# Folding each batch's memory values into the first mixture's weights, with attention weights as its input

## The chip, the cores and the metric

One Trainium2 chip, one of its cores. The metric is the device time of one execution in microseconds. An execution of this kernel has five engines at work: TensorE (PE, with its weight loads shown as PEld), VectorE (DVE), ScalarE (ACT), GpSimd (POOL), and SyncE (SP), which here only issues transfers.

## The reference, cut to what matters

Three parts follow each other: a memory attention of 4 batches of 576 tokens (8 heads of 64), a gated mixture layer of 1536 columns over all 2304 tokens, and a second layer that sends every token to two of eight experts.

```python
a = softmax(phi)                                   # 32 memories per head
k_m = einsum('bhsm,bhsd->bhmd', a, k)
v_m = einsum('bhsm,bhsd->bhmd', a, v)
attn = softmax(q @ k_m.T / 8)                      # tokens x 32 memories, per head
x = (attn @ v_m).transpose(0, 2, 1, 3).reshape(2304, 512)
x = (sigmoid(x @ w_gate) * (x @ w_val)) @ w_out    # first mixture
x = top2_experts(x)                                # second mixture
```

With 8 heads of 32 memories, the attention weights of a token are 256 numbers; the values that they are multiplied with differ from batch to batch only. Nothing non-linear stands between `attn @ v_m` and the two products with `w_gate` and `w_val`.

## The kernel before, in words

Numbers that stand for fp32 are kept as two f16 parts, hi and lo, and a product is three f16 matmuls (hi hi, hi lo, lo hi). The parts come from `split` (line 391): a ScalarE copy with a scale (392) and a VectorE subtraction (393).

*Attention* (lines 166 to 315) works batch by batch in fp32: `memory` builds the keys and values of the memories, four heads beside each other on the array (187), `scores` and `turned` the attention weights with their tokens on the columns (244, 265), `result` the product with the values (278, 285), whose hi and lo are `xT[b]` (288, 289), 512 rows by 576 tokens. Attention is a generator, `atts`; the main loops take a step of it after each piece of their own work.

*Weights* (343 to 389) arrive as 64-bit words, 36 halves of 512 KB through four buffers, and are put together by ScalarE, VectorE and GpSimd (337 to 341). Gate and value weights are split into hi and lo, 12 blocks of 128 x 1024 (`finish`, 350 to 358). Those of w_out are split last (385 to 389), after all have been summed.

*First product*, `stage1` (426 to 453): for a chunk c of 256 tokens and a tile f of 128 columns, 2 x 12 matmuls of up to 256 columns (442) into one PSUM buffer of four (`pg`), where chunks that straddle a batch are cut in two. Then Tanh on ScalarE (448), a VectorE step (449), a ScalarE copy (451) and a VectorE subtraction (452) give gT in hi and lo. There are 9 x 12 calls.

*Second product*, `stage2` (455 to 464): for each tile T of 128 tokens 36 matmuls of 512 columns into `px`. `tokens` (466) then scales and stores the row, transposes it by a transfer (482, 485), multiplies it with the router (492) and, for every second tile, `route` (546) computes the choice and scatters it to the table `meta` (608).

*Order in `build`* (989 to 1079): the first three chunks of the first product are computed beside the weights, 36 calls; then come the second product of chunk 0 and, in turn, a call of the first product and a third of a tile of the second (1057 to 1068). Presplits of the first experts' weights (632 to 677) run beside it once attention is done, and are drained before the last chunk. After chunk 6 the routing is frozen for the first three tiles of expert 0 (615 to 623), which are fetched, gathered and transposed (755 to 777, 814) under the last chunk's first product. The end of the first mixture is two second products (1072), the early rows' matmuls (1074), and the fetch of the late rows (1079, 1080). A scheduler orders the instructions of each engine at build time by priority and dependence.

*Second mixture*, `moe2`, lines 786 and 800, isn't touched.

Of the kernel before, what the change touches and what calls it, by code (L numbers as in the profile page):

```python
# [26 lines left out]
P = 128  # L27
# [5 lines left out]
NCH = N // CH  # L33
NT = N // P
# [12 lines left out]
FB = 8  # L47
SG = 3

STEPS = 3  # L50

GT = 36
WAIT_W, WAIT_SPLIT, WAIT_TURN, WAIT_ROUTE = 2, 4, 5, 4
WAIT_TURN_LAST, WAIT_ROUTE_LAST = 4, 2
# [7 lines left out]
class Kern:  # L62
# [12 lines left out]
    def norm2(self, pool, m, tag, before=1, n=1):  # L75
# [11 lines left out]
        nc.vector.tensor_scalar(h, pt.bitcast(I32), 24, 23, op0=ALU.logical_shift_right, op1=ALU.logical_shift_left)  # L87
        nc.vector.tensor_scalar(s, h, -1, 204 << 23, op0=ALU.mult, op1=ALU.add)
# [3 lines left out]
    def consts(self):  # L92
# [10 lines left out]
        self.idle = cp.tile([P, 256], F16, name="idle")  # L103
        nc.vector.memset(self.idle, 0.0)
        self.ones = cp.tile([P, P], F16, name="ones")
        nc.vector.memset(self.ones, 1.0)

    def warm(self, n):

        nc = self.nc  # L110
        pt = self.pg.tile([P, 512], F32, tag="pg", name="pw")
        for i in range(n):
            d = nc.tensor.matmul(pt[:, :256], self.ones, self.idle, start=True, stop=True)
            self.tc.add_manual_dep(d.ins, self.mark.ins.name, mybir.DependencyInfo(mybir.DependencyClass.NoSync, mybir.DependencyReason.DATA), reason="order")
            self.mark = d


    def att_open(self):
        tc, nc = self.tc, self.nc
        self.att_ctx = ExitStack()  # L120
        pool = lambda name, bufs: self.att_ctx.enter_context(tc.tile_pool(name=name, bufs=bufs, side="left"))
        self.stage = pool("stage", 4)
        self.a1 = pool("a1", 1)
        self.a2 = pool("a2", 2)
        self.kbds = [self.a1.tile([P, 4, 64], F32, name=f"kbd{i}") for i in range(1)]
        self.vbds = [self.a1.tile([P, 4, P], F32, name=f"vbd{i}") for i in range(1)]
        for t in self.kbds + self.vbds:
            nc.gpsimd.memset(t, 0.0)
        self.al, self.ag = {}, {}

    def att_load(self, b, what, g):
# [5 lines left out]
        else:  # L137
            if what == "q" and b == 0:
                t = self.flat(self.xp.tile([P, KT, S], F16, tag=f"x{g}", name=f"x{g}")).bitcast(F32)
            else:  # L140
                t = self.stage.tile([P, (SC + 1) * 256], F32, tag="st", name="st")
            if what == "q":
                t = t[:, : 2 * S].rearrange("p (t s) -> p t s", t=2)
                src = a["q"][b * DM : (b + 1) * DM, :].rearrange("(g t p) s -> g p t s", p=P, g=2)[g]
# [21 lines left out]
    def memory(self, b, g):  # L166

        nc, a2, al = self.nc, self.a2, self.al
        kbd, vbd = self.kbds[0], self.vbds[0]
# [18 lines left out]
        km = a2.tile([P, 2, D], F32, tag="km", name="km")  # L188
        nc.scalar.copy(km, pm[:, :D].unsqueeze(1).to_broadcast([P, 2, D]))
        for j in range(4):  # L190
            rows = slice(32 * j, 32 * j + 32)
            nc.scalar.copy(vbd[rows, 2 * g + j // 2, (j % 2) * 64 : (j % 2) * 64 + 64], pm[rows, D:])
# [3 lines left out]
        pk = self.pg.tile([P, 512], F32, tag="pg", name="pa")[:, :P]  # L196
        nc.tensor.transpose(pk, km.rearrange("p a d -> p (a d)"), self.idf)
        pk = pk.rearrange("p (a b) -> p a b", a=2)
        for j in range(2):
            rows, cols = slice(64 * j, 64 * j + 64), slice(32 * j, 32 * j + 32)  # L200
            nc.scalar.copy(kbd[rows, 2 * g : 2 * g + 2, cols], pk[rows, :, cols])
# [18 lines left out]
    def values_scale(self, b):  # L220
        m = self.a2.tile([P, 1], F32, tag="vm", name="vm")
        self.xT[b] = [self.xp.tile([P, KT, S], F16, tag=f"x{i}", name=f"x{i}") for i in range(2)]
        junk = self.xT[b][0][:, 0, :512].bitcast(BF16)
        self.nc.scalar.activation(junk, self.flat(self.vbds[0]), AF.Square, accum_out=m)
        self.sv[b], iv = yield from self.norm2(self.cp, m, f"sv{b}")
        self.invx.append(iv)

    def attention(self, b):

        nc, a2, al, sv = self.nc, self.a2, self.al, self.sv[b]  # L230
        kbd, vbd = self.kbds[0], self.vbds[0]
        qt = [al[(b, "q", g)] for g in range(2)]
        def scores(u):
# [3 lines left out]
            for pr in range(2):  # L237
                cols = slice(pr * 64, pr * 64 + 64)
                if u == 2:
                    for g in range(2):  # L240
                        nc.tensor.matmul(ps[SH * g : SH * (g + 1), 0, cols], qt[g][:, pr, SC * P :], kbd[:, 2 * g + pr, :], start=True, stop=True)
                else:
                    for t in range(SC):
                        self.mark = nc.tensor.matmul(ps[:, t, cols], qt[u][:, pr, t * P : (t + 1) * P], kbd[:, 2 * u + pr, :], start=True, stop=True)  # L244
# [15 lines left out]
        def turned(u, ex):  # L260
# [3 lines left out]
            for t in range(nt):  # L264
                d = nc.tensor.transpose(pt[:, t, :], at[:, t, :], self.idf)
                if b == u == 0:
                    self.tc.add_manual_dep(d.ins, self.mark.ins.name, mybir.DependencyInfo(mybir.DependencyClass.NoSync, mybir.DependencyReason.DATA), reason="order")
                self.mark = d
            th = a2.tile([P, SC * P], F32, tag="th", name="th")[:, : nt * P]
            nc.scalar.copy(th, pt[:, :nt, :].rearrange("p a b -> p (a b)"))  # L270
            return th

        def result(u, th):
            if u == 2:
                po = self.pg.tile([P, 4, P], F32, tag="pg", name="pa")[:, :, :SH]
                for g in range(2):
                    for pr in range(2):
                        nc.tensor.matmul(po[:, 2 * g + pr, :], vbd[:, 2 * g + pr, :], th[:, g * SH : (g + 1) * SH], start=True, stop=True)
                outs = [(po, [x[:, :, SC * P :] for x in self.xT[b]])]
            else:  # L280
                outs = []
                for pr in range(2):
                    po = self.pg.tile([P, SC * P], F32, tag="pg", name="pa")
                    half = slice(64 * pr, 64 * pr + 64)
                    self.mark = nc.tensor.matmul(po, vbd[half, 2 * u + pr, :], th[half, :], start=True, stop=True)  # L285
                    outs.append((po, [x[:, 2 * u + pr, : SC * P] for x in self.xT[b]]))
            for po, (oh, ol) in outs:
                nc.scalar.activation(oh, po, AF.Copy, scale=sv)
                nc.vector.scalar_tensor_tensor(ol, po, sv, oh, op0=ALU.mult, op1=ALU.subtract)
        self.gs[b] = {}  # L290
        ex, th = {}, {}
# [3 lines left out]
        if b == 0:  # L295
            self.warm(20)
        for i in range(2):
            th[i] = turned(i, ex[i])
            yield
            if b + 1 < B:  # L300
                for x in ((("phi", 0), ("phi", 1), ("kv0", 0)), (("kv1", 0),))[i]:
                    self.wanted.append((b + 1, *x))
        for i in range(2):
            result(i, th[i])
            yield
# [5 lines left out]
        th = turned(2, ex)  # L311
        yield
        result(2, th)
# [29 lines left out]
    def weights(self):  # L343
# [3 lines left out]
        blocks = self.wgv + self.wob  # L347
        sums = {}

        def finish(u, wait=WAIT_W):  # L350

            s, iv = yield from self.norm2(cp, sums[u], f"w{u}", wait, 2)
            for j in range(2):
                n = 2 * u + j
                (self.iwv if j else self.iwg).append(iv[:, j : j + 1])
# [766 lines left out]
```

## Time and profile before

| | us |
|---|---|
| median of 3 runs | 980.79 |
| lowest, highest | 976.62, 983.88 |
| span of the profiled execution | 977.2 |
| TensorE, VectorE, ScalarE, GpSimd busy in it | 929.4, 470.2, 468.8, 213.2 |

The profiled execution is known by its span, from its first to its last instruction; the three times are of whole executions and lie within 7 us of it. Stretches below are counted from the span's start. A group of instructions gives a line, an engine, what is written and read, and the mean of one; a matmul's record is longer than its step, since matmuls are pipelined, so a price per matmul is taken from the length of an unbroken run divided by its count.

### The profile page before, as it was taken

What the parts mean: (1) busy time and instruction counts of PE and PEld (TensorE: products, weight loads), DVE (VectorE), ACT (ScalarE), POOL (GpSimd) and SP (SyncE); (2) the same over time, 40 slices, a digit from 0 to 9 for tenths busy, and PEclk for the clock granted to TensorE, in tenths of its full rate; (3) what the DMA queues carried; (4) which work ended last, traced back from release to release, by engine and by line L of the source; (5) the groups of instructions that cost most, each with busy time, mean ns of one, the idle gap of its engine ahead of it and who ended that gap; (6) DMA issues with size and microseconds to landing.
All of it is one profiled execution on the core that took longest, in us unless ns stands there. A gap on an engine that the chain in (4) does not pass through costs nothing.

```text
span 977.2 us, 18935 instructions
## 1 busy us (share of the span) xinstructions
PE 929.4 (95%) x7567; PEld 646.0 (66%) x7567; DVE 470.2 (48%) x1286; ACT 468.8 (48%) x979; POOL 213.2 (22%) x211
## 2 busy tenths in 40 slices
PE   6769899999999999999999989999999999999995
PEld 5457679766678877887776547657474756565662
DVE  2889974224543555567542514735354544432110
ACT  4778774234435344556431416746364646543230
POOL 1553520001011001020202054033232323141102
PEclk9779989999999999999999999999999999999998
DMA  8588574043122005474616949457757676645303
GB/s 301 182 251 263 177 257 142 12 95 105 22 71 72 23 19 187 128 234 141 199 26 149 362 110 205 177 129 124 203 118 206 112 184 134 162 81 78 41 12 43
DMA packets 125898, 135.28 MB, mean 138 GB/s; under 512 B 71792, under 2 KB 88304, under 8 KB 125296
## 3 DMA queue, kind: packets, MB, share of 16 engines
q1 hardware_dynamic: 115824, 113.30, 40.1%
q0 software_dynamic: 9984, 20.75, 11.8%
q8 instruction: 60, 0.98, 0.4%
q14 instruction: 30, 0.25, 0.1%
HBM read 87.97 MB, written 30.86 MB: 122 GB/s over the span
## 4 chain that ended last, share of the span: by engine, by line
PE 85%; DMA 4%; DVE 4%; ACT 3%; issue 1%; POOL 1%; SPq 0%; POOLq 0%; ACTq 0%; DVEq 0%
PE pg L442 26%; PE ph L786 20%; PE py L800 19%; PE px L464 14%; PE pa L244 1%; PE pa L187 1%; DMA w<-wo 1%; DVE w L393 1%; ACT w L375 1%; PE pa L285 1%; DMA xe<-xg 1%; PE pl L492 1%; DMA xt<-row 1%; DVE pw L339 1%; DMA w<-wv 1%
## 5 line engine op out<-in xcount | busy, mean ns | idle before, releaser
L442 PE MATMUL pg<-x,w 128*128 128x256 f16 (+3 forms) x3456 | 308.2, 249 | 8.7 <-ACT w L392 5.2
L442 PEld LDWEIGHTS <-w 128*128 128x128 f16 x3456 | 271.5, 100 | 40.1 <-issue 7.0
L800 PEld LDWEIGHTS <-hT 128*128 128x128 f16 (+1 forms) x960 | 100.0, 105 | 105.2 <-DVE hT L792 1.0
L464 PE MATMUL px<-wo,gT 128*128 128x512 f16 x648 | 146.8, 379 | 0.0
L806 POOL DMA_INDIRECT out<-y,mts x40 | 63.8, 1595 | 230.2 <-ACT y L805 229.0
L786 PE MATMUL ph<-xe,w1a 128*128 128x312 f16 (+2 forms) x768 | 105.0, 299 | 3.6 <-DMA xe<-xg 3.6
L464 PEld LDWEIGHTS <-gT 128*128 128x128 f16 x648 | 62.2, 98 | 66.9
L800 PE MATMUL py<-w2a,hT 128*128 128x512 f16 (+1 forms) x480 | 105.0, 379 | 0.1
L800 PE MATMUL py<-w2b,hT 128*128 128x512 f16 (+1 forms) x480 | 104.7, 379 | 0.0
L786 PE MATMUL ph<-xe,w1b 128*128 128x312 f16 x768 | 102.8, 296 | 0.0
L608 POOL DMA_INDIRECT meta<-mt,vi x36 | 36.7, 1020 | 292.6 <-DVE vi L605 207.3
L448 ACT ACTIVATE sg<-pg,gs 128x256 f32<-128x256 f32 (+3 forms) x144 | 56.1, 416 | 92.4 <-PE pg L442 91.1
L792 DVE TENSOR_TENSOR hT<-r,hT 128x312 f16<-128x312 f32 (+2 forms) x128 | 56.6, 478 | 83.8 <-ACT hT L791 83.3
L786 PEld LDWEIGHTS <-w1a 128*128 128x128 f16 x768 | 75.8, 99 | 31.3 <-DMA xe<-xg 4.1
L786 PEld LDWEIGHTS <-w1b 128*128 128x128 f16 x768 | 75.2, 98 | 26.8
L449 DVE SCALAR_TENSOR_TENSOR pg<-sg,pg 128x256 f32<-128x256 f32 x108 | 45.8, 424 | 90.3 <-ACT sg L448 90.1
L805 ACT ACTIVATE y<-py,css 128x512 f32<-128x512 f32 (+1 forms) x40 | 27.5, 687 | 127.7 <-PE py L800 123.2
L790 ACT ACTIVATE r<-ph 128x312 f32<-128x312 f32 (+2 forms) x128 | 48.9, 428 | 78.9 <-PE ph L786 74.5
L451 ACT ACTIVATE gT<-pg 128x256 f16<-128x256 f32 x108 | 41.0, 380 | 44.6 <-DVE pg L449 44.2
L771 POOL DMA_INDIRECT xg<-xs,mts x40 | 46.7, 1167 | 67.4 <-DMA mts<-meta 26.6
L452 DVE SCALAR_TENSOR_TENSOR gT<-pg,gT 128x256 f16<-128x256 f32 x108 | 45.4, 420 | 26.7 <-ACT gT L451 26.6
L791 ACT CAST hT<-r 128x312 f16<-128x312 f32 (+2 forms) x128 | 52.4, 460 | 0.4
(310 smaller groups left out, 886.2 us busy)
## 6 DMA issues: line engine op xcount, KB each, us to landing
wo<-w SPq DMA_DIRECT2D x48, 512.0 KB, 5.4
st<-kv SPq DMA_DIRECT2D x16, 512.0 KB, 5.3
f<-w SPq DMA_DIRECT2D x16, 512.0 KB, 6.4
wsp<-hl SPq DMA_DIRECT2D x16, 512.0 KB, 3.2
w<-wg SPq DMA_DIRECT2D x12, 512.0 KB, 5.3
w<-wv SPq DMA_DIRECT2D x12, 512.0 KB, 4.8
w<-wo SPq DMA_DIRECT2D x12, 512.0 KB, 4.1
out<-z SPq DMA_DIRECT2D x23, 256.0 KB, 3.7
```

The source lines that it names most:

```text
L442: nc.tensor.matmul(pg[:, j, s:e], w[:, l, k, fo : fo + P], self.xT[b][r][:, k, t0 : t0 + e - s], start=n == 0, stop=n == 3 * KT - 1)
L448: nc.scalar.activation(sg[:, s:e], pg[:, 0, s:e], AF.Tanh, scale=self.gate_scale(b, u))
L449: nc.vector.scalar_tensor_tensor(pg[:, 1, :], sg, 1.0, pg[:, 1, :], op0=ALU.add, op1=ALU.mult)
L452: nc.vector.scalar_tensor_tensor(g[:, 1, :], pg[:, 1, :], 2.0 ** -16, g[:, 0, :], op0=ALU.mult, op1=ALU.subtract)
L464: nc.tensor.matmul(p, g[:, l, t * P : (t + 1) * P], self.wob[f // 2][:, r, f % 2, :], start=f + i == 0, stop=f == FT - 1 and i == 2)
L771: self.nc.gpsimd.indirect_dma_start(out=xg.rearrange("p a b -> p (a b)"), out_offset=None, in_=self.xs[:rows, :], in_offset=bass.IndirectO ...
L786: nc.tensor.matmul(p[:, : t1 - t0], w1[:, l, k, f * P : (f + 1) * P], xe[:, x, t0:t1], start=n == 0, stop=n == 3 * KT - 1)
L790: nc.scalar.activation(r, p[:, : t1 - t0], AF.Relu, scale=2.0 ** -19)
L791: nc.scalar.copy(self.hT[:, 0, f, t0:t1], r)
L792: nc.vector.tensor_sub(self.hT[:, 1, f, t0:t1], r, self.hT[:, 0, f, t0:t1])
L800: nc.tensor.matmul(py, self.hT[:, l, f, i * P : i * P + m], w2[:, w, f, :], start=n == 0, stop=n == 3 * F2T - 1)
L806: d = nc.gpsimd.indirect_dma_start(out=self.out, out_offset=bass.IndirectOffsetOnAxis(ap=mt[:m, 0:1], axis=0), in_=y[:m], in_offset=None, ...
```

## The change

`x = attn @ v_m` is no longer formed. `fold(b, u)` multiplies the values of batch b, kept for the pairs of heads as four blocks of 128 x 64, into the 256 columns u of w_gate and w_val, in fp32, and splits the product into hi and lo (`wq`). `stage1(b, u, ch)` multiplies that with the attention weights, 256 rows instead of 512 (`xT[b]`, hi and lo, written straight from the transposed weights), for chunks of 192 tokens, three to a batch; a call does two tiles f, 24 matmuls of 192 columns into two PSUM buffers, and reads out 384 columns in a step. The gate and value weights stay in fp32 (`W`) and aren't split. There are 24 folds and 72 calls.

The order of the loops changes with it: beside the weights only batch 0 is done; then, for b = 1, 2, 3, the second products of the tiles that are complete (T 0 to 2, 3 to 8, 9 to 11) are followed by that batch's six folds and 18 calls; the last six second products (T 12 to 17) end the first mixture. The routing is frozen after tile 13, in those six. Attention b may start its `memory` once batch b - 2 has been folded. `GT` is 12 buffers of 384 tokens by 256 columns, `FB` 6 instead of 8, and 20 matmuls on constants (`warm`) go.

```diff
+QC = 192
+BLK = 384
-FB = 8
-SG = 3
-GT = 36
+FB = 6
+SG = 2
+GT = 12
+WQ = 4
-WAIT_TURN_LAST, WAIT_ROUTE_LAST = 4, 2
+WAIT_TURN_LAST, WAIT_ROUTE_LAST = 3, 3
...
+    def fold(self, b, u):
+
+        nc = self.nc
+        vbd = self.vbds[b % 2]
+        s = self.cp.tile([P, 2], F32, tag="ws", bufs=4, name="ws")
+        nc.vector.tensor_scalar(s, self.sw[u], self.sv[b], 2.0 ** -A_BITS, op0=ALU.mult, op1=ALU.mult)
+        t = self.wq[(b, u)] = self.wqp.tile([P, 2, 2, 2, 256], F16, tag="wq", name="wq")
+        for g in range(2):
+            pv = self.pg.tile([P, 2, 256], F32, tag="pg", name="pv")
+            for j in range(2):
+                for pr in range(2):
+                    rows, k = slice(64 * pr, 64 * pr + 64), 2 * g + pr
+                    nc.tensor.matmul(pv[rows, j, :], vbd[:, k, :], self.W[2 * u + j][:, k, :], start=True, stop=True, tile_position=(0, 64 * pr))
+            for j in range(2):
+                self.split(pv[:, j, :], s[:, j : j + 1], t[:, 0, g, j, :], t[:, 1, g, j, :])
...
-        if b == 0:
-            self.warm(20)
...
-            for j in range(2):
-                n = 2 * u + j
-                (self.iwv if j else self.iwg).append(iv[:, j : j + 1])
-                self.split(self.flat(blocks[n + 1]).bitcast(F32), s[:, j : j + 1], self.flat(blocks[n][:, 0]), self.flat(blocks[n][:, 1]))
-                self.wdone = n + 1
-                yield
+            self.sw.append(s)
+            self.iwg.append(iv[:, 0:1])
+            self.iwv.append(iv[:, 1:2])
+            yield
...
+    def stage1(self, b, u, ch):
+
...
+        ps = [self.pg.tile([P, 512], F32, tag="pg", name="pg")[:, : 2 * QC].rearrange("p (f s) -> p f s", f=2) for _ in range(2)]
+        for j, p in enumerate(ps):
+            for f in range(2):
+                n = 0
+                for g in range(2):
+                    for l, r in ((0, 0), (0, 1), (1, 0)):
+                        nc.tensor.matmul(p[:, f, :], w[:, l, g, j, f * P : (f + 1) * P], x[:, r, g, ch * QC : (ch + 1) * QC], start=n == 0, stop=n == 5)
+                        n += 1
+        sg = self.sp.tile([P, 2, QC], F32, tag="sg", name="sg")
+        nc.scalar.activation(sg, ps[0], AF.Tanh, scale=self.gate_scale(b, u))
+        pv = ps[1]
+        nc.vector.scalar_tensor_tensor(pv, sg, 1.0, pv, op0=ALU.add, op1=ALU.mult)
+        nc.scalar.activation(o[:, 0, :, cols], pv, AF.Copy, scale=2.0 ** -16)
+        nc.vector.scalar_tensor_tensor(o[:, 1, :, cols], pv, 2.0 ** -16, o[:, 0, :, cols], op0=ALU.mult, op1=ALU.subtract)
...
+        for b in range(1, B):
...
+            second(*range(3 * (b - 1) // 2 * TB, 3 * b // 2 * TB))
+            if b == B - 1:
+                while pre is None:
+                    beside()
                 drain(pre)
...
+            self.fold(b, 0)
+            for u in range(UN):
+                if u + 1 < UN:
+                    self.fold(b, u + 1)
+                for ch in range(S // QC):
+                    first(b, u, ch)
+                    beside()
+            self.folded = b + 1
...
+        second(*range(3 * (B - 1) // 2 * TB, NT))
+        while not rows or rows[0] in side:
+            beside()
```

ScalarE, in a stretch of first products: before, in the turn of first and second products (sg is Tanh of line 448, gT the copy of 451, the other rows belong to attention, tokens and presplits):

```order
L448 ACTIVATE sg_4934<-pg_4909,gs22_3992 128x256
L451 ACTIVATE gT_4937<-pg_4909 128x256
L270 COPY th_5023<-pa_5021 128x128
L480 ACTIVATE row_5085<-px_4718,tts_5080 128x512
L448 ACTIVATE sg_4992<-pg_4967,gs23_4157 128x256
L288 ACTIVATE x0_4504<-pa_5056,sv3s_4580 128x4x64
L451 ACTIVATE gT_4995<-pg_4967 128x256
L448 ACTIVATE sg_5050<-pg_5025,gs23_4157 128x256
```

The same in the changed kernel, in batch 1's pass (wq is the hi part of a fold, from its PSUM buffer pv):

```order
L377 ACTIVATE wq_2401<-pv_2402,ws_2399 128x256
L377 ACTIVATE wq_2401<-pv_2411,ws_2399 128x256
L377 ACTIVATE wq_2401<-pv_2402,ws_2399 128x256
L377 ACTIVATE wq_2401<-pv_2411,ws_2399 128x256
L428 ACTIVATE sg_2446<-pg_2420,gs12_2447 128x384
L431 ACTIVATE gT_985<-pg_2421 128x2x192
L428 ACTIVATE sg_2510<-pg_2484,gs12_2447 128x384
L431 ACTIVATE gT_2483<-pg_2485 128x2x192
L428 ACTIVATE sg_2541<-pg_2515,gs12_2447 128x384
L431 ACTIVATE gT_2483<-pg_2516 128x2x192
```

Each sg has 384 columns instead of 256, its gT stands between it and the next sg, and four copies of a fold precede three calls.

SP, at the end of the first mixture: before (mts is the fetched table, xe the early rows' transposes, xs and xt a tile's row and its transpose, wo the loads of later experts):

```order
L759 DMA mts_7242<-meta_116 128x6
L777 DMA_TRANSPOSE xe_6889<-xg_7275 128x8x128
L777 DMA_TRANSPOSE xe_6889<-xg_7277 128x8x128
L777 DMA_TRANSPOSE xe_6889<-xg_7279 128x8x128
L753 DMA w2a_7484<-wsp_117 128x8192
L482 DMA xs_115<-row_7508 128x1024
L485 DMA_TRANSPOSE xt_7513<-row_7508 128x8x128
L753 DMA w1b_7483<-wsp_117 128x8192
L482 DMA xs_115<-row_7561 128x1024
L485 DMA_TRANSPOSE xt_7566<-row_7561 128x8x128
```

The same in the changed kernel:

```order
L738 DMA mts_5891<-meta_119 128x6
L674 DMA wo0_71<-w1 128x1024
L461 DMA xs_118<-row_5995 128x1024
L464 DMA_TRANSPOSE xt_6000<-row_5995 128x8x128
L674 DMA wo1_72<-w1 128x1024
L756 DMA_TRANSPOSE xe_4745<-xg_5905 128x8x128
L756 DMA_TRANSPOSE xe_4745<-xg_5907 128x8x128
L756 DMA_TRANSPOSE xe_4745<-xg_5909 128x8x128
L674 DMA wo2_73<-w1 128x1024
L674 DMA wo3_74<-w1 128x1024
L461 DMA xs_118<-row_6073 128x1024
L464 DMA_TRANSPOSE xt_6078<-row_6073 128x8x128
```

Before, three tiles' transposes (two of them shown) stand behind the early rows; now it is the last tile's alone, row_6073, and the early rows stand behind the row of tile 16.

## Rows read from the trace of the kernel before

**Rows 1.** The page: busy time of the engines; TensorE in 40 slices.

```profile
PE 929.4 (95%) x7567; PEld 646.0 (66%) x7567; DVE 470.2 (48%) x1286; ACT 468.8 (48%) x979; POOL 213.2 (22%) x211
...
PE   6769899999999999999999989999999999999995
```

**Rows 2.** Busy time by stretch: length, each engine's busy us, clock, DMA share.

```profile
30.00:138.00 108.00, 85.57 (x708) 66.27 (x709) 93.45 (x202) 84.54 (x169) 52.88 (x62) 0.83 0.72 227
138.00:183.00 45.00, 45.00 (x650) 43.11 (x647) 21.97 (x42) 22.19 (x52) 0.00 (x0) 1.00 0.43 146
183.00:546.00 363.00, 362.30 (x3498) 266.17 (x3497) 176.00 (x604) 148.73 (x324) 39.87 (x51) 1.00 0.37 108
546.00:584.00 38.00, 33.21 (x219) 17.79 (x218) 14.16 (x80) 13.90 (x28) 14.27 (x14) 1.00 0.70 207
```

**Rows 3.** The chain that ended last: start us, us, what.

```profile
183.29 15.56 PE px L464 x72
198.85 2.62 PE pg L442 x24
...
210.23 1.36 PE pa L187 x40
211.59 2.62 PE pg L442 x23
...
266.42 1.11 PE pa L285 x4
...
293.99 2.68 PE pg L442 x48
...
578.25 5.45 DMA xe<-xg
583.75 11.68 PE ph L786 x96
```

**Rows 4.** Groups of instructions by form: busy us, mean ns of one.

```profile
L464 PE MATMUL px<-wo,gT 128*128 128x512 f16 x648 | 146.8, 379 | 0.0
...
L452 DVE SCALAR_TENSOR_TENSOR gT<-pg,gT 128x256 f16<-128x256 f32 x108 | 45.4, 420 | 26.7 <-ACT gT L451 26.6
...
L451 ACT ACTIVATE gT<-pg 128x256 f16<-128x256 f32 x108 | 41.0, 380 | 44.6 <-DVE pg L449 44.2
...
L448 ACT ACTIVATE sg<-pg,gs 128x256 f32<-128x256 f32 x72 | 33.5, 470 | 52.6 <-PE pg L442 51.4 <-PE pl L492 0.8
...
L792 DVE TENSOR_TENSOR hT<-r,hT 128x384 f16<-128x384 f32 x8 | 4.4, 553 | 2.0 <-ACT hT L791 2.0
...
L790 ACT ACTIVATE r<-ph 128x384 f32<-128x384 f32 x8 | 3.9, 484 | 3.7 <-PE ph L786 3.6
```

**Rows 5.** The same from 183.2 to 546.4 us: the result matmuls.

```profile
L285 PE MATMUL pa<-th,vbd 64*128 64x512 f32 x16 | 5.4, 635 | 0.7 <-DVE x L289 0.7
...
L278 PE MATMUL pa<-th,vbd 128*128 128x64 f32 x16 | 2.1, 271 | 0.0
```

**Rows 6.** Stretch before w_out's splits: line 393 alone, then line 449 alone.

```profile
0.00:136.70 136.70, 20.13 (x12) 0.86 0.72 230
...
0.00:137.90 137.90, 7.54 (x18) 0.86 0.72 231
```

**Rows 7.** Timeline around w_out's first splits.

```profile
136.74 1.15 ACT L392 ACTIVATE wo<-wo,wos 128x1024 f16<-128x1024 f32 x1
...
137.92 1.28 DVE L393 SCALAR_TENSOR_TENSOR wo<-wo,wos,wo 128x1024 f16<-128x1024 f32 x1 [0.46 <-ACT wo L392]
```

**Rows 8.** Timeline of the snapshot's rows and of the end of the second product.

```profile
512.36 0.96 POOL L608 DMA_INDIRECT meta<-mt,vi  x1 [39.11 <-DVE vi L605]
...
524.68 4.43 SPq L777 DMA_TRANSPOSE xe<-xg  x3
...
546.38 0.69 DVE L476 TENSOR_REDUCE am<-px 128x1 f32<-128x512 f32 x1 [5.01 <-PE px L464]
...
555.47 0.45 PE L492 MATMUL pl<-wr,xt 128*128 128x16 f16 x12
```

More of the change, by code (lines that the diff above doesn't have):

```diff
@@ L187, in memory @@
                 self.mark = nc.tensor.matmul(pm[rows, :], ag[:n, c, rows], kv[j // 2][:n, c, j % 2, :], start=c == 0, stop=c == SC, tile_position=(0, 32 * j))
[L188 to L192, printed above, removed]
+        km = a2.tile([P, 2, 2, D], F32, tag="km", name="km")
+        nc.scalar.copy(km, pm.rearrange("p (x d) -> p x d", x=2).unsqueeze(2).to_broadcast([P, 2, 2, D]))
         if g == 0 and b:
@@ L264, in turned @@
             for t in range(nt):
[L265 to L273, printed above, removed]
-            if u == 2:
[L275 to L279, printed above, removed]
-            else:
[L281 to L289, printed above, removed]
+                self.mark = nc.tensor.transpose(pt[:, t, :], at[:, t, :], self.idf)
+            if u == 2:
+                src = pt[:, 0, :].rearrange("p (g s) -> p g s", g=2)
+                oh, ol = (x[:, l, :, SC * P :] for l in range(2))
+            else:
+                src = pt.rearrange("p a b -> p (a b)")
+                oh, ol = (x[:, l, u, : SC * P] for l in range(2))
+            nc.scalar.activation(oh, src, AF.Copy, scale=2.0 ** A_BITS)
+            nc.vector.scalar_tensor_tensor(ol, src, 2.0 ** A_BITS, oh, op0=ALU.mult, op1=ALU.subtract)
         self.gs[b] = {}
-        ex, th = {}, {}
+        ex = {}
         for i in range(2):
@@ L970, in attend @@
             yield from self.features(b)
+            while self.folded < b - 1:
+                yield
             yield from self.memory(b, 0)
@@ L1028, in build, with beside @@
         self.router_open()
[L1030 to L1038 removed]
+        pre, rows = None, []
+        def beside():
+            nonlocal pre
             step()
[L1040 to L1042 removed]
+            turns(atts)
             if pre is None and self.attended == B:
@@ L1048, in build, with second @@
                 pre = start(self.presplits())
-            if c == NCH - 1:
+            if self.snapped and not self.mt:
+                self.fetch(0, 0, EARLY, self.scatters)
+                rows.append(start(self.early_rows()))
+        def second(*Ts):
+            for T in Ts:
+                for fs in (range(0, 4), range(4, 8), range(8, 12)):
+                    self.stage2(T, list(fs))
+                    beside()
+                g = start(self.tokens(*divmod(T, CH // P)))
+                if T >= NT - CH // P:
+                    offset[g] = AHEAD
+        for b in range(1, B):
[3 more added lines that the diff above has]
+                    beside()
                 drain(pre)
@@ L1056, in build @@
                 self.xe_tile(0)
-            for f in range(GT - 3 * FT if c == 3 else 0, FT):
-                first(c, f)
-                step()
-                turns(atts)
-                if f % 2 or c == 3:
-                    next(nxt, None)
-                    step()
-                if self.snapped and not self.mt:
-                    self.fetch(0, 0, EARLY, self.scatters)
-                    start(self.early_rows())
-            for _ in nxt:
-                step()
+            self.fold(b, 0)
+            for u in range(UN):
+                if u + 1 < UN:
+                    self.fold(b, u + 1)
+                for ch in range(S // QC):
+                    first(b, u, ch)
+                    beside()
+            self.folded = b + 1
         mw.close()
```

206 lines of the change are left out of this document (78 added, 128 removed).

## The prediction

> **What bounds the kernel now.** I read the page first, then the busy time by stage, then the chain that ended last, then single groups and stretches.
>
> The page shows TensorE busy for 95% of the span, and its slices are at eight tenths or more except the first three and the last [rows 1]. An average hides the stages, so the stretches matter [rows 2]. From 30 to 138 us TensorE is busy 85.6 of 108 us at a mean granted clock of 0.83, while VectorE works 93.5 and ScalarE 84.5: here the weights are being prepared and TensorE waits for them. From 138 to 183 us it is busy all of the 45 us: a backlog of first-mixture matmuls is worked off, with the weights long there. From 183 to 546 us it is busy 362.3 of 363 at full clock: every matmul taken out there counts. From 546 to 584 us the second mixture's first rows are awaited, a chain of transfers with filler on TensorE. After 584 us nothing is touched by the change.
>
> The chain says the same in order of time [rows 3]: from 183 us on the second product (line 464) in turn with the first (line 442), and at 578 us a transfer, xe, that lands before the late part begins at 583.75.
>
> **The change, part by part.**
>
> *First product.* Before, a call makes 24 matmuls of 256 columns: 2.62 us, or 109 ns each. Where a call straddles a batch in halves, 48 matmuls of 128 columns take 2.68 us, 56 ns each [rows 3]. 192 columns lie midway: 82.5 ns, and a call of 24 is 1.98 us. There were 108 calls and there will be 72, because the sum now runs over 256 rows and not 512. In the stretch from 183 us on there are 72 calls before (189 us) and 54 after (107 us).
>
> *Result matmuls.* The product of attention weights and values goes: for the two batches in that stretch 5.4 + 2.1 = 7.5 us [rows 5]. A few transposes of the values come in its place; I leave them out as small.
>
> *Fold, the added work.* Each of 24 folds makes eight fp32 matmuls of 256 columns, each on half of the array's columns, two beside each other. The trace of before doesn't show this form; two rows lie on either side. Line 187 is fp32 with 128 columns, four beside each other: 40 records (20 matmuls) in 1.36 us, 0.27 us for a set of four. Line 285 is fp32 with 512 columns, two beside each other: 1.11 us for the pair [rows 3]. Between 128 and 512 columns a straight line gives 0.55 us at 256, and twice line 187's set 0.54. I take 0.54 us a pair, 2.17 us a fold, 39 us for the 18 folds in the long stretch. Bounds: from below four f16 steps of 109 ns a pair, 1.74 us a fold (the 512-column pair, 1.11 us, is above four of line 464's 216 ns); from above pairs that don't overlap at all, 4.3 us. That is 31 to 78 us.
>
> Fp32 work with part of the columns stands between ordinary matmuls without a gap in the trace: line 187 starts at 210.23 us, lasts 1.36, and line 442 goes on at 211.59 [rows 3]. The Trainium skill, "TensorEngine Tiling (Array Packing)", Key Properties, says that changing the tiling mode drains TensorE, which speaks against 24 more changes there and back. As an estimate, a drain is a record's length less its step, 379 − 216 = 163 ns for line 464 [rows 3, 4]; 18 folds with two changes each would add 5.9 us to the sum by that rule. The trace shows no such gap, so the sum has none.
>
> *Reading out.* A call now evicts 384 columns instead of 256. The copy and the two VectorE steps are taken as 0.484 and 0.553 us from the 384-column rows of lines 790 and 792; against the 256-column copy's 0.380 that is 0.104 more, so Tanh goes from 0.470 to about 0.574 us. A fold adds four copies and four subtractions at about 0.38 and 0.42 us [rows 4]. Three calls and a fold are then 8.1 us of TensorE against 3 × 1.06 + 4 × 0.38 = 4.7 us of ScalarE and 3 × 1.11 + 4 × 0.42 = 5.0 us of VectorE. That hides, but thinner than before: first and second product no longer alternate in a batch's pass, a call holds two of the four PSUM buffers where it held one, and in the third pass the presplits queue on the same two engines (the ScalarE rows of the order show it: four wq, then sg and gT in strict turn). Behind a late gT on ScalarE stands the next sg, and for that the matmuls two calls on wait. For what that loses, with the drained presplits ahead of the last batch, I put 15 us; bounds are 0 (before, TensorE lost under 1 us in 363 [rows 2]) and 40.
>
> *First stretch.* The stage-two matmuls can't begin before the first split of w_out, whose copy starts at 136.74 and whose subtraction ends at 139.2 us; a split's copy waits for the subtraction ahead of it, so the six come about 1.15 + 1.28 us and a few tenths apart [rows 7]. T0 and T1 now go side by side, twelve matmuls (2.6 us) for each split, and keep pace with that. Before, 45 us of backlog stood in front; now b = 0 needs only 18 calls, 36 us, and six folds, 13 us at full clock, beside the weights. What moves the first split: VectorE loses 12 splits of gate and value weights, 20.1 us, gains 24 subtractions of folds, 10.1 us, and 18 calls at 1.11 instead of 18 at 0.84 us (7.54 us for 18 of one of the two steps) add 4.9 [rows 6]. Net 5 us less on the busiest engine. I take 138 (that subtraction's start, 137.92) − 5 = 133 us as the effective start of the second product. Bounds 125 (ScalarE's relief counts too) and 146 (no relief, and TensorE starting at the low clock it has in this stretch).
>
> *The end of the first mixture.* Before, three early tiles of expert 0 were routed, gathered and transposed under first-product matmuls. After, tiles 12 to 17 are the last six second products in a row, and the snapshot's routing (pk) stands in T16, 13.9 us ahead of their end. From pk to the first scatter takes some 3 us; scatter to first transpose was 512.36 to 524.68, 12.3 us; the third transpose is issued 3 us later and lands 5.45 us after [rows 3, 8]. So early rows are there 3 + 12.3 + 3 + 5.5 − 13.9 = 10 us after the last second product; before they were waiting. On SP the last token's transpose stands behind those three (order rows). Its router matmul, 555.47 − 546.4 = 9.1 us after the end before [rows 8], stands behind some 4.7 us of early matmuls: about 15 us, 6 later. The rest, 583.75 − 546.4 = 37.4 us, moves with it: 43.4 us. Bounds 37 and 52.
>
> *Sum.* The long stretch, 183.3 to 546.4 us: 363.1 − 189 − 7.5 + 107 + 39 = 312.6 us, plus 15. From the profiled execution's own span: 133 + 327.6 + 43.4 + (977.2 − 583.8 = 393.4) = 897.4 us, 79.8 less than 977.2. That span lies near the lower end of the three times shown (976.62, 980.79, 983.88), so I take the difference off the median: 901.
>
> **Rivals.**
>
> *Folds one after the other.* If the halves don't overlap, 18 × 2.17 = 39 us more: 940. For it: two-wide forms are not in the trace. Against: the four-wide one shows overlap.
>
> *The start doesn't come earlier.* The first stretch is bound by transfers as well (DMA share 0.72 [rows 2]), and TensorE idles more there, so second products begin at 146: 914. This is the case in which 45 us of backlog were partly hidden.
>
> *Gain beyond the sum.* No stall, start at 125, folds at their lower bound: 901 − 15 − 8 − 8 = 870.
>
> *Read-out bounds each call: slower.* Two PSUM buffers a call and four in all: if the buffers come free so late that each call waits out its own last three steps, 0.553 + 0.484 + 0.553 = 1.59 us, and each fold its last pair, 0.80 us, the price is 54 × 1.59 + 18 × 0.80 = 100 us, and the time 1001. It decides from 79.8 / 54 = 1.5 us a call on. Against it: the buffer that call n + 2 needs last is wanted 2.9 us after call n's end, and its chain is 1.6 us and the semaphores. For it: ScalarE's FIFO with the presplits in it. The Trainium skill's same page, PSUM Bottleneck, says that tiling speeds up TensorE but not the reading of PSUM, which may become the bound; it would make this case likelier in the folds, but the rows give 3.2 us of slack for every three calls.
>
> *The change doesn't shorten TensorE's work.* It would need the first product to be hidden; 45.0 of 45 and 362.3 of 363 us busy exclude it.
>
> **How the numbers follow.** The forecast, 885 to 912, has 0.62; the start that isn't earlier 0.13; the serial folds 0.10, half of them short of full price; the larger gain 0.11; the slower case 0.03; 0.01 for no change by several of these at once. The range of 8 in 10 is 872 to 932: the forecast's own, the late start, part of the serial folds and most of the larger gain. About 1% is what these runs, 0.4% apart on either side, can tell from no change; below 971 is faster: 0.96, within 1% 0.01, slower 0.03.
>
> **What would show it.** Right: first second product at about 133 us with no block of line-442 work ahead of it; folds of about 2.2 us; calls of 1.98 us in unbroken turn; TensorE over 95% busy between; a gap of some 10 us before the early rows' matmuls. Wrong: folds of over 3.5 us, waits of TensorE on gT or wq of more than 30 us in sum, a start after 145 us, or a late part more than 52 us behind the last second product.

## The result, and the profile after

The changed kernel takes 899.77 us (median of 4 runs, 895.88 to 901.81) against 981.93 us before (4 runs): a ratio of 0.9169, 95% interval 0.9132 to 0.9206. Later, beside three of the experiments, it was 901.86 us (6 runs, 899.23 to 907.93; ratio 0.9207, interval 0.9171 to 0.9244). The forecast was 901, within 872 to 932. So the sum held; its terms did so less well, and their errors, up to 5 us each, nearly cancel. One of the runs below, 935.2 us with the folds doubled, was in a slower state; without it that kernel's median is 924.0 us.

The page of the changed kernel, engines and TensorE's slices, answers to [rows 1]:

```profile
PE 826.5 (92%) x6147; PEld 541.2 (60%) x6147; DVE 471.7 (53%) x1317; ACT 452.5 (50%) x917; POOL 210.0 (23%) x212
...
PE   5469789999999999999959999999999999999995
```

TensorE has 103 us less to do, ScalarE 16 us less, VectorE and GpSimd about as much as before. The one thin slice in the middle (5) is the end of the first mixture.

Busy time by stretch, in the columns of [rows 2]: beside the weights, from the first second product to the last, from there to the late part, the late part.

```profile
30.00:138.00 108.00, 80.14 (x751) 62.60 (x752) 87.80 (x228) 80.89 (x171) 51.31 (x62) 0.86 0.74 232
...
138.00:457.10 319.10, 312.79 (x2713) 210.96 (x2713) 207.72 (x663) 160.65 (x320) 38.45 (x50) 1.00 0.48 146
...
457.10:504.30 47.20, 35.28 (x202) 17.99 (x201) 12.92 (x72) 12.49 (x25) 15.52 (x17) 0.86 0.62 147
504.30:898.30 394.00, 381.89 (x2353) 236.25 (x2353) 153.25 (x324) 186.23 (x373) 101.13 (x71) 0.99 0.60 126
```

The 45 us of backlog are gone, and second products run from 138 us on, with TensorE shown idle for 6.3 us of the next 319. The end of the first mixture is longer than the 37.4 us of before, at a mean clock of 0.86 where it was 1.00. The late part is what it was.

TensorE's timeline at the places the prediction speaks of: the first second products, three calls between two folds, a fold ahead of six calls, the snapshot (line 597), the last second product, the early rows and the late part.

```profile
138.02 0.59 PE L443 MATMUL px<-wo,gT 128*128 128x512 f16 x2 [0.55 <-ACT wo L377]
...
152.62 15.25 PE L443 MATMUL px<-wo,gT 128*128 128x512 f16 x69 [0.77 <-DVE wo L378]
...
204.18 6.11 PE L425 MATMUL pg<-x,wq 128*128 128x192 f16 x72
210.22 1.95 PE L240 MATMUL pv<-w,vbd 128*64 128x256 f32 x16
...
400.35 1.95 PE L240 MATMUL pv<-w,vbd 128*64 128x256 f32 x16
402.23 12.05 PE L425 MATMUL pg<-x,wq 128*128 128x192 f16 x144
414.12 12.68 PE L443 MATMUL px<-wo,gT 128*128 128x512 f16 x58
...
443.65 0.16 PE L597 MATMUL pk<-oacc,ones 128*1 128x1 f16 x1
...
451.48 5.34 PE L443 MATMUL px<-wo,gT 128*128 128x512 f16 x24
...
467.27 7.52 PE L765 MATMUL ph<-xe,w1a 128*128 128x384 f16 x29 [8.35 <-DMA xe<-xg]
474.63 0.45 PE L471 MATMUL pl<-wr,xt 128*128 128x16 f16 x12
474.94 5.36 PE L765 MATMUL ph<-xe,w1a 128*128 128x384 f16 x32
...
504.34 10.01 PE L765 MATMUL ph<-xe,w1a 128*128 128x240 f16 x96 [1.84 <-DMA xe<-xg]
```

A fold is 1.88 us from its start to the next call's (400.35 to 402.23), and six calls are 11.89 us (402.23 to 414.12): 1.98 each. Three calls that end at a fold take 6.04 us (204.18 to 210.22), 0.09 more than half of that. The last second product ends at 451.48 + 5.34 = 456.8 us, the early rows' matmuls start 10.5 us later, the last tile's router matmul 17.8 and the late part 47.5.

The six splits of w_out on ScalarE, first and last, against [rows 7]:

```profile
136.81 1.16 ACT L377 ACTIVATE wo<-wo,wos 128x1024 f16<-128x1024 f32 x1
...
152.60 1.15 ACT L377 ACTIVATE wo<-wo,wos 128x1024 f16<-128x1024 f32 x1 [2.25 <-DVE wo L378]
```

The first one hasn't moved: 136.81 us against 136.74. The six come 3.2 us apart (15.79 / 5), where 2.6 were expected.

### The profile page after: what moved, and what is told of

It is laid out like the page before. It is cut to its first block, busy times and chain, and to the rows that moved or that the text cites. A ratio compares the mean times of both kernels' runs of the same rounds, so it can differ in the third digit from the quotient of the medians.

```text
span 898.3 us, 16054 instructions
## 1 busy us (share of the span) xinstructions
PE 826.5 (92%) x6147; PEld 541.2 (60%) x6147; DVE 471.7 (53%) x1317; ACT 452.5 (50%) x917; POOL 210.0 (23%) x212
## 3 DMA queue, kind: packets, MB, share of 16 engines
q0 software_dynamic: 9984, 20.75, 13.2%
## 5 line engine op out<-in xcount | busy, mean ns | idle before, releaser
L425 PE MATMUL pg<-x,wq 128*128 128x192 f16 x1728 | 163.9, 254 | 14.8 <-ACT wq L377 8.3
L425 PEld LDWEIGHTS <-wq 128*128 128x128 f16 x1728 | 147.4, 101 | 32.1 <-ACT wq L377 15.0
L765 PEld LDWEIGHTS <-w1b 128*128 128x128 f16 x768 | 75.2, 98 | 28.6 <-issue 1.9
L782 DVE TENSOR_TENSOR css<-mts,iw 128x1 f32<-128x1 f32 (+1 forms) x40 | 6.6, 166 | 90.6 <-ACT y L784 88.5
L431 ACT ACTIVATE gT<-pg 128x384 f16<-128x384 f32 x72 | 35.2, 488 | 34.8 <-DVE pg L430 34.6
L432 DVE SCALAR_TENSOR_TENSOR gT<-pg,gT 128x384 f16<-128x384 f32 x72 | 40.0, 555 | 22.1 <-ACT gT L431 21.7
L240 PE MATMUL pv<-w,vbd 128*64 128x256 f32 x384 | 49.1, 396 | 2.5 <-POOL wo L334 1.8
```

The lines of the kernel that those rows point to most:

```text
L240: nc.tensor.matmul(pv[rows, j, :], vbd[:, k, :], self.W[2 * u + j][:, k, :], start=True, stop=True, tile_position=(0, 64 * pr))
L425: nc.tensor.matmul(p[:, f, :], w[:, l, g, j, f * P : (f + 1) * P], x[:, r, g, ch * QC : (ch + 1) * QC], start=n == 0, stop=n == 5)
L432: nc.vector.scalar_tensor_tensor(o[:, 1, :, cols], pv, 2.0 ** -16, o[:, 0, :, cols], op0=ALU.mult, op1=ALU.subtract)
L765: nc.tensor.matmul(p[:, : t1 - t0], w1[:, l, k, f * P : (f + 1) * P], xe[:, x, t0:t1], start=n == 0, stop=n == 3 * KT - 1)
```

## The experiments

Each profile below is one execution, and the first stretch of an execution can differ by some us with nothing changed (last section). So the profiles are compared by the time from the last split of w_out to the end of the last second product ("stretch"), and from there to the late part ("tail"):

| kernel | median us (runs) | ratio to before, interval | last split | stretch | tail |
|---|---|---|---|---|---|
| changed kernel | 899.8 (4) | 0.9169, 0.9132 to 0.9206 | 152.6 | 304.2 | 47.5 |
| the same again | 901.9 (6) | 0.9207, 0.9171 to 0.9244 | 152.6 | 304.3 | 49.2 |
| folds twice | 926.6 (4) | 0.9425, 0.9351 to 0.9500 | 142.5 | 336.3 | 45.5 |
| folds one half after the other | 916.0 (4) | 0.9303, 0.9219 to 0.9388 | 155.2 | 320.1 | 45.6 |
| weights' splits back | 916.9 (4) | 0.9312, 0.9251 to 0.9374 | 168.0 | 309.7 | 44.0 |
| tile 12 ahead | 902.2 (4) | 0.9143, 0.9075 to 0.9212 | 147.3 | 308.3 | 46.7 |
| copy twice | 898.9 (6) | 0.9193, 0.9153 to 0.9234 | 148.9 | 307.7 | 46.9 |
| ring of five | 903.8 (6) | 0.9167, 0.9124 to 0.9211 | 153.8 | 306.5 | 49.9 |
| first chunk ahead | 904.4 (6) | 0.9219, 0.9182 to 0.9257 | 150.9 | 312.4 | 38.5 |
| matmuls on constants | 899.8 (6) | 0.9170, 0.9143 to 0.9197 | 151.6 | 305.8 | 44.2 |
| first chunk ahead, turns later | 903.4 (6) | 0.9156, 0.9112 to 0.9199 | 153.4 | 317.1 | 36.3 |
| that and the constants | 900.1 (6) | 0.9145, 0.9099 to 0.9191 | 147.4 | 316.4 | 36.1 |
| that and the loads later | 893.8 (6) | 0.9042, 0.9000 to 0.9084 | 154.0 | 307.9 | 37.8 |

The runs come from five sets, in which the kernel before had medians from 980.4 to 988.4 us; so ratios compare better than medians. Tile 12 ahead and copy twice, whose last split came 4 to 5 us early, have a stretch some 3.5 to 4 us longer. TensorE is shown idle in it for 8.4 and 7.3 us, against 4.9 in the changed kernel, the longest waits being for sg (1.8 us) and for the routing (2.4 us). Ring of five, whose split wasn't early, has a wait of 1.7 us for sg too. Why they come isn't shown, so differences of a stretch under 4 us are left unread.

**What a fold costs.** In `fold`:

```diff
-            for j in range(2):
+            for j in [0, 1] * 2:
```

> Every matmul of a fold is issued twice into the same columns, so a fold has 16 instead of 8; nothing else changes and nothing is read twice. Theory (TensorE bounds the long stretch, and a fold costs it what the trace of the changed kernel shows, 1.87 us): the 18 folds from 168 us on cost 18 x 1.87 = 34 us more, the six beside the weights little, so the time goes from 899.8 to 930 to 940, and a fold's run of 16 matmuls lasts 3.7 us. Rival (a fold costs TensorE little because around it TensorE would wait for its copies anyway): under 10 us more.

Two folds in a row of this kernel, and one:

```profile
283.01 7.13 PE L240 MATMUL pv<-w,vbd 128*64 128x256 f32 x64
...
296.69 3.67 PE L240 MATMUL pv<-w,vbd 128*64 128x256 f32 x32
```

16 more matmuls are 7.13 − 3.67 = 3.46 us, 1.73 us for the eight of a fold. The stretch is 32.1 us longer, 28.6 against that of copy twice (307.7), which had an early split too: for 18 folds 1.6 to 1.8 us each. A fold is paid in full on the path. The median rose by 22 to 27 us, less than the expected 30 to 40; in the profiled execution, the fastest of the four, the first stretch was shorter (last split at 142.5 us).

**Whether its halves run beside each other.** Both PSUM buffers at the start, then:

```diff
+        for pr in range(2):
+            for g, pv in enumerate(pvs):
+                for j in range(2):
```

> The same eight matmuls of a fold in another order: the four of one half of the array's columns first, then the four of the other half, instead of in turn; both PSUM buffers are taken at the start and read out after all eight. Theory (neighbours on different halves run beside each other, which is why a fold took 1.87 us and not double): in the new order only the two at the seam can overlap, seven steps of 0.47 us instead of four, 3.3 us a fold; 18 x 1.4 = 25 us more, 920 to 930. Rival (they ran one after the other already, 0.235 us each): the same within 4 us.

```profile
211.00 2.86 PE L240 MATMUL pv<-w,vbd 128*64 128x256 f32 x16
213.79 6.12 PE L426 MATMUL pg<-x,wq 128*128 128x192 f16 x72
```

A fold is 2.79 us here from its start to the next call's, against 1.88: 18 × 0.91 = 16.4 us, and the stretch is 15.9 longer. So neighbours on different halves do overlap. But the median, 916.0 us, stays under the expected 920 to 930: 3.3 us a fold would need a matmul alone to take as long as a pair. From first to next it is 2.79 / 8 = 0.35 us alone and 1.88 / 4 = 0.47 us for a pair: the overlap saves a third, not half.

**What sets the first split of w_out.** In `weights`, after each gate or value block:

```diff
+            if kind != "wo":
+                self.split(v, 1.0, self.flat(self.wob[0][:, 0]), self.flat(self.wob[0][:, 1]))
```

> The splits of the gate and value weights come back beside the weights as idle work: 12 copies of 1024 columns on ScalarE and 12 subtractions on VectorE, about 14 and 15 to 20 us, whose results nobody reads. The prediction's step (VectorE's busy time sets when w_out's first split comes): the second product starts 15 to 20 us later than at 138 us, and the time is 915 to 920. Rival (the weights' arrival through their four buffers sets it; the first split came at 136.8 us in both kernels although VectorE had 7 us less to do): the start moves by under 4 us and the time by under 5.

The first split comes at 152.59 us, 15.8 later, and the median rises by 15 to 17 us (by the ratios, 10 to 14). So work added on VectorE and ScalarE there is paid almost one for one, as the prediction's step has it; which of the two engines counts wasn't separated. Yet taking out 5.7 us net of VectorE's work (93.45 to 87.80 us between 30 and 138) moved nothing.

```diff
-WB = 4
+WB = 5
```

> Five buffers instead of four for the weights' 64-bit halves; nothing else. Theory (w_out's first split waits for work in order on ScalarE and VectorE, to which 12 idle splits added 16 us, not for the transfers): the last load is issued earlier but the first split moves by under 3 us from 136.6 us, and the time stays within 4 us of 901.9. Rival (the ring of four sets the start: the last two loads were issued at 117.6 and 120.3 us only when a buffer came free): the first split at 128 to 132 us, the time 894 to 898.

The last weight load is issued at 116.86 us and not at 120.34, and the first split comes at 138.34: the ring of buffers isn't it. What holds the start where it was, with less work on both engines, was not singled out. A candidate, not tried by itself, are the six folds of batch 0, a new step between weights and first product: of the changed kernel's waits (us in total, times, longest) one of the largest on TensorE, all of it ahead of 138 us, is for their copies. Their matmuls are less likely: with these doubled, the first split came at 127.80 us.

```profile
PE pg L425 <- ACT wq L377: 8.3, 5, 4.0
```

**Whether reading out PSUM bounds a call.** The copy to gT is issued twice:

```diff
         nc.scalar.activation(o[:, 0, :, cols], pv, AF.Copy, scale=2.0 ** -16)
+        nc.scalar.activation(o[:, 0, :, cols], pv, AF.Copy, scale=2.0 ** -16)
```

> The copy of a call's result to gT is issued twice on ScalarE, so each call's chain from PSUM grows by 0.49 us and the buffer comes free that much later. Theory (the reading out hides under the next call's 1.98 us): at most 3 us more in sum, TensorE's waits in the long stretch still under 10 us. Rival (four PSUM buffers, two a call, make each call wait for its chain): 54 x 0.49 = 26 us more.

The stretch is 3.4 us longer, as it is with tile 12 ahead, which leaves the reading out alone, and the median 3 us lower than that of the same kernel again: nothing. The slower rival is excluded by its own price.

**Where the end's 47 us come from.** First, tile 12 ahead of batch 3's pass:

```diff
-            second(*range(3 * (b - 1) // 2 * TB, 3 * b // 2 * TB))
+            second(*range(3 * (b - 1) // 2 * TB, 3 * b // 2 * TB + (b == B - 1)))
```

> The second product of tile 12, complete after batch 2, is computed ahead of batch 3's pass instead of at the end; five instead of six tiles end the first mixture, and the snapshot's routing falls one tile earlier. Theory (the early rows come late since the snapshot stands only one tile ahead of the end): their matmuls start some 7.8 us nearer to the last second product, TensorE's wait of 8.35 us for them shrinks to 1 us or so, the last tile's router matmul no longer stands behind them, and the late part starts 5 to 9 us earlier: 891 to 895. Rival (the chain of the last tile, its transpose, routing, fetch and gather, sets the late part's start by itself): the wait moves but the late part starts 47 us after the last second product as now, 899 to 900.

Nothing changed, and it tells neither theory apart: the snapshot follows tile 13, and four tiles follow tile 13 in either order. Its matmul of line 597 stood 13.2 us ahead of the end, as in the changed kernel. The expectation had overlooked that. What moves it is first-product work behind tile 13:

```diff
-                for ch in range(S // QC):
+                for ch in range(S // QC if u < split else 1):
...
+            if b == B - 1:
+                second(12, 13)
+                for u in range(split, UN):
+                    for ch in (1, 2):
+                        first(b, u, ch)
+                        beside()
...
+        second(14, 15, 16, 17)
```

> In batch 3's pass the first chunk of all column blocks comes first (the first two blocks whole), then the second products of tiles 12 and 13, then the other eight calls, and four instead of six tiles at the end. So tile 13's routing, the snapshot, stands some 30 us ahead of the last second product and not 13. Theory (TensorE's 8.35 us of waiting for the early rows, and the last tile's router matmul 17.5 us after the end because it stands behind them, come from the snapshot's place): no wait for early rows, the router matmul 8 to 10 us after the last second product, the late part 38 to 41 us after it instead of 47: 891 to 894. Rival (the last tile's chain of transfers takes 47 us by itself): the wait moves to before the late rows, 899 to 901.

The tail is 38.5 us, as the theory said, but the median doesn't fall: the stretch grew by 8 us. TensorE waited 6.3 us there for tile 14's transpose, xt. On SP it stood behind the early rows' transposes, which waited for their gathers. Four steps more before those transposes (the expectation says three):

```diff
-        yield
-        yield
+        for _ in range(6):
+            yield
```

> The kernel with batch 3's first chunk ahead, and in it the three early transposes are issued three steps later on SP, behind tile 14's row and not ahead of it. Theory (what that kernel won in the tail, 38.5 us instead of 47 to 49, it gave back where TensorE waited 6.3 us for tile 14's transpose, which stood on SP behind the early transposes' wait for their gathers): no wait over 2 us for a tile's transpose, the late part still 38 to 40 us behind the last second product, 890 to 896. Rival (the transposes and gathers get in each other's way on the transfer engines wherever they stand): the wait comes back at another tile, 898 to 904.

The wait stays, 5.0 us, though xt now goes first. TensorE and SP there:

```profile
444.80 4.48 PE L443 MATMUL px<-wo,gT 128*128 128x512 f16 x20
454.32 0.49 PE L471 MATMUL pl<-wr,xt 128*128 128x16 f16 x12 [5.04 <-DMA xt<-row]
```

```profile
442.03 0.43 SPq L732 DMA_DIRECT2D w1b<-wsp  x1
442.56 0.37 SPq L461 DMA_DIRECT2D xs<-row  x1
443.03 4.14 SPq L464 DMA_TRANSPOSE xt<-row  x1
450.97 4.60 SPq L756 DMA_TRANSPOSE xe<-xg  x3
```

The transpose lands 11.3 us after its issue (443.03 to 454.32). In front of it on SP went the 2 MB load of w1b, whose buffer comes free with the first mixture's weights and which isn't read before expert 1. The Trainium skill, "DMA: Bandwidth & Descriptors", Queues, rings and completion order, says that within one issuing engine's queue each DMA engine takes its descriptors in order; these rows and the next agree. With the matmuls on constants (below) added, the picture was the same:

> The last one and the 26 and 20 matmuls on constants. Theory (the two don't touch each other): 2 us under the last one at most, 889 to 895, since the matmuls on constants didn't bring the full clock to the scores. Rival (the matmuls delay the first attention): 1 to 3 us over it.

It came to 900.1 us, with a wait of 6.4. Last, the loads of expert 1's weights behind the last tile's transpose:

```diff
-        self.wload2(1, 0)
-        self.wload2(1, 1)
+        self.wload2(1, 0, self.last_xt)
+        self.wload2(1, 1, self.last_xt)
```

> The last one, and the two 2 MB loads of expert 1's weights (w1b, w2b) are issued on SP behind the last tile's transpose; before, w1b was issued in front of tile 14's row and its transpose landed 11 us after its issue. Theory (what the earlier snapshot wins in the tail was given back to that load): no wait of TensorE over 2 us for a tile's transpose, the end of the second product 5 to 7 us earlier after the last split of w_out than in the last two, the late part 38 to 41 us behind it: 892 to 896. Rival (the transposes are late for another reason, as their own place on SP): the wait of 5 to 6 us stays, 899 to 903.

TensorE and SP at the same place:

```profile
439.78 8.58 PE L455 MATMUL px<-wo,gT 128*128 128x512 f16 x39
448.20 0.45 PE L483 MATMUL pl<-wr,xt 128*128 128x16 f16 x12
```

```profile
441.08 0.42 SPq L473 DMA_DIRECT2D xs<-row  x1
441.62 1.29 SPq L476 DMA_TRANSPOSE xt<-row  x1
```

The transpose is there within 6.6 us of its issue and nothing waits for it; the stretch is 307.9 us and the tail 37.8. The median is 893.8 us, ratio 0.9042, and the upper end of its interval, 0.9084, lies under the lower ends of both measurements of the changed kernel and, by little, under that of the kernel without this edit, 0.9099: the best version of the study. That the two loads' place matters is shown by this pair of kernels, which differ in nothing else.

**The clock at the start.** 26 matmuls on constants before the first attention step and 20 after its first product:

```diff
+        with ahead_by(2 * AHEAD):
+            self.warm(26)
...
+        if b == 0:
+            self.warm(20)
```

> 26 matmuls on constants before the first attention step, while TensorE waits for the softmax until 7.5 us, and 20 after the first scores, as in the kernel before. Theory (in some executions the first stretch runs 4 to 6 us late because batch 0's 32 score matmuls take 7.2 us instead of 3.9, TensorE being at its lower clock there): the scores take 3.9 us in this profile, the second product starts at 129 to 133 us, and the median is 3 to 6 us under the changed kernel's, with less scatter. Rival (the weights' transfers catch up any delay): second product at 136 to 138 us and the same time.

The theory failed at its first step: the first attention matmuls took 7.2 us again (3.51 and 3.65 for 16 records each). The first split came at 135.98 us, and the median is 2 us lower, with intervals that overlap, as the rival has it. What the short records would be worth, this run can't tell. What it shows of the clock stands in the last section.

## Why the prediction was right, term by term

The forecast for the profiled execution was 897.4 us and its span is 898.3. By terms:

| term | forecast us | measured us |
|---|---|---|
| end of the last second product | 133 + 327.6 = 460.6 | 456.8 |
| from there to the late part | 43.4 | 47.5 |
| late part to the end | 393.4 | 394.0 |

*What bounds it.* Right. TensorE bounds the long stretch: a call is 1.98 us as forecast from half way between two rows, a doubled fold costs its whole length, a doubled copy nothing.

*The start.* The term "138 − 5 = 133" failed. The first split came at 136.81 us, and the first second product's matmuls at 138.02; until 152.6 us they keep pace with the splits. The step priced each microsecond of VectorE's work as one of the start. The splits put back show that for work added (15.8 us later), but the relief of 5.7 us on VectorE gave nothing; why stays open. Like is compared with like here: before, batch 0's first attention matmuls had the long records of the last section too:

```profile
20.18 4.51 PE L244 MATMUL pa<-kbd,x 128*128 128x64 f32 x20
```

Four profiles of the changed kernel's start have long ones as well, and their first split lies between 134.9 and 137.7 us. In the one with short ones (tile 12 ahead) the second product began at 132.6: the forecast's 133, but not by the forecast's cause.

*The fold.* Right in kind, 0.29 us too dear: 1.88 and not 2.17 us, for 18 folds 5.2 us. Eight more of its matmuls cost 1.73 us, the prediction's lower bound (1.74); the straight line between 128 and 512 columns was a quarter too high (0.54 us a pair against 0.43). What comes on top goes with the change to half of the columns and back: 1.88 − 1.73 = 0.15 us in the fold and 0.09 in front of it. For 15 places, since two of a batch's six folds stand in a row, that is 3.6 us. The Trainium skill's rule that a change of the tiling mode drains TensorE ("TensorEngine Tiling (Array Packing)", Key Properties) agrees with that; the 5.9 us weighed for it were not far off. The reason to leave it out, that the trace shows no gap, was a reading of the chain alone; the timeline of before has one:

```profile
209.96 0.27 PE L442 MATMUL pg<-x,w 128*128 128x256 f16 x1
210.16 1.43 PE L187 MATMUL pa<-st,a 128*32 128x128 f32 x40
```

From the start of the one matmul to that of the next 0.20 us pass and not 0.109, and the record of 0.27 us covers that.

*Stalls.* 15 us were put down. As idle time 6.3 are there (319.10 − 312.79), none of them over 1.0 us at once. But a matmul's record is longer than its step (line 443: 379 ns against 216), so each pause hides some 0.16 us, and a shorter one hides whole. Counted in the trace from each matmul's start to the next one's start, between the first second product and the last, line 443 takes 147.0 us where 648 × 0.216 is 140.0, line 425 takes 110.1 where 1296 × 0.0825 is 106.9, and the folds 35.9 where 18 × 1.88 is 33.8: 12.3 us more, so the term was near. About 2 us of it lie beside w_out's splits. The doubled copy shows that the buffers of PSUM are no bound.

The stretch adds up: 312.6 − 5.2 + 12.3 = 319.7 us, where 456.8 − 138.0 = 318.8 were needed. That the whole came within 1 us of the forecast is luck: the start's 5 us and the end's 4.1 to the bad stand against 5.2 of the folds and 2.7 of the stalls to the good.

*The end.* The early rows came 10.5 us after the last second product, 10 were forecast. The last tile's router matmul came 17.8 us after it and not 15: in front of it stood 7.4 us of early matmuls (467.27 to 474.63), and not 4.7. They were 29 matmuls of 384 columns, 0.25 us each, while the next 32 took 0.17 (5.36 us): TensorE had idled 8.35 us before the first, and its granted clock was lower under them than under the next (the columns of [rows 2], where it was 1.00):

```profile
467.30:474.90 7.60, 7.60 (x40) 3.89 (x41) 0.56 (x1) 1.85 (x4) 0.30 (x1) 0.65 1.02 311
474.90:481.00 6.10, 5.42 (x41) 3.10 (x38) 3.72 (x22) 4.48 (x11) 0.00 (x0) 1.00 0.10 35
```

From the router matmul to the late part it is 29.7 us, before 28.3. Sum: 4.1 us more.

*The rivals.* Serial folds: excluded by their own experiment, and their price, 39 us, was too high: 16. Reading out: excluded. The late start: 5 of its 13 us happened, in the first split; the waits behind it were under 1 us each. The larger gain didn't, though the folds' matmuls came at their lower bound.

## What to carry to other kernels

When one engine is busy without a gap, price a change by its unbroken runs on that engine, divided by their count: those terms came within a sixth here. Count pauses from start to start, since records longer than their steps hide them: idle time showed half of what was lost. A term that credits less work on an engine with an earlier start needs the chain of waits behind it: here work added moved the start and work taken out did not. Near the end of a stage look at what the queue of transfers carries in front of a small, awaited one: early 2 MB loads that nobody needed yet took back 8 us which a better order had won.

## What was not expected of the hardware

The first stretch differs between executions of one program. Batch 0's first attention matmuls (fp32, 64 columns), in the changed kernel and in the kernel with tile 12 ahead, which is the same up to there:

```profile
18.54 4.37 PE L260 MATMUL pa<-kbd,gT 128*128 128x64 f32 x20
```

```profile
17.53 2.34 PE L260 MATMUL pa<-kbd,gT 128*128 128x64 f32 x20
```

The same 20 records take 4.37 or 2.34 us, about the ratio of the clock's two levels, 1.2 and 2.4 GHz. After the short records the first split of w_out came at 131.35 us, after the long ones at 136.81, and at 136.57 in the changed kernel's second profile, with 4.36 us for the 20. The other kernels agree: 127.8 to 132.7 us in three more with short ones, 134.9 us or later in all with long ones. It may be part of the 6 to 14 us by which runs of one kernel differ; only the profiled ones can be looked into.

Work ahead doesn't make it sure. In the kernel with matmuls on constants TensorE worked from 1.35 us on. The 26 took 5.70 us, 0.22 each, where a step of 256 columns is 0.109; the attention records behind them are short ones until 13 us; then, between 16 and 27 us, with TensorE busy 10.48 of 11 us, the granted clock is 0.50:

```profile
1.35 5.70 PE L117 MATMUL pw<-idle,ones 128*128 128x256 f16 x26 [1.35 <-DVE ctr L872]
...
18.36 3.51 PE L270 MATMUL pa<-kbd,gT 128*128 128x64 f32 x16
```

```profile
16.00:27.00 11.00, 10.48 (x64) 9.18 (x57) 2.94 (x9) 2.90 (x9) 0.00 (x0) 0.50 0.66 245
```

In the kernel that adds the chunk order, with the same beginning, those 16 records took 1.90 us; with the loads later, 3.51 again. For the changed kernel the column gives 1.00 in that same stretch beside the 4.37 us above, so there the durations are the safer guide.
